# Two edits to the matmul order of a fused attention and two mixtures of experts: a weight maximum moved behind its diagonal, and branches around the slots that may hold no token

## The chip, the cores and the metric

One core of a Trainium2 chip. TensorE (PE) multiplies into PSUM, VectorE (DVE) and ScalarE (ACT) work element by element, GpSimd (POOL) subtracts and issues the scatters by index, SyncE (SP) issues the other DMAs. Each engine runs its own instructions in order and waits for the others by semaphores. The metric is the device time of one execution in microseconds; lower is better.

## The reference

```python
def _attn_ref(u, v, z):                       # batch 4, 2496 tokens, 256 wide, z 64 wide
    scores = (1.0 / S) * np.matmul(z, z.transpose(0, 2, 1))
    return u * np.matmul(np.maximum(scores, 0.0) ** 2, v)

def _moe_ref(x, w_gate, w_output_gate, w1, w2):   # 9984 tokens, 8 experts, 1024 hidden
    logits = x @ w_gate; e_idx = np.argmax(logits, axis=1)
    # gate_w: the chosen expert's softmax probability; eom: sigmoid(x @ w_output_gate)
    for e in range(E):
        mask = e_idx == e
        out[mask] = gate_w[mask, None] * eom[mask, e, None] * (np.maximum(x[mask] @ w1[e], 0.0) @ w2[e])
```

`reference` is the attention, then this first mixture of experts (MoE), then a second one of the same shape without the output gate. How many tokens go to an expert is known only while the kernel runs.

## The kernel before

**Slots.** A MoE gathers its tokens by expert into tiles of 128 rows. There are 9984 = 78 x 128 tokens, and each of 8 experts may leave a last tile part empty, so the program holds 85 slots (`SLOTS`), enough for any split. The first 64 are taken in 32 pairs of full tiles; slots 64 to 84 are single tiles. Three maps (a, b and c) are computed on the chip by `map_stages`: for each unit the row at which its tokens start and the offset of its expert's weights. PE and SP load these numbers into registers (`want_pe`, `get_sp`). A slot past the last tile has expert number 8: the offset is clamped to a valid expert, its rows are padding rows, and its scatter has only indices out of bounds, which write nothing.

**Steps.** A slot has two products. `g1` (x times W1) makes `hp`, from which ACT (relu, line 1303) and DVE (the rounding rest, line 1304) make HB in two float16 parts. `g2` (HB times W2) makes `yp`. A pair's g1 has two parts of 24 matmuls of 256 columns, a single's g1 is 48 matmuls of 128 columns, and a g2 is 24 matmuls of 256 columns. All add three products of float16 parts. `order`, written out by the loop at line 1558, alternates g1 and g2, with g1 ahead by up to 12 slots. In the first MoE eight g1 stand in a row before the last fifteen g2; in the second the last ten g2 stand alone. `hp` (tag "s") and `yp` (tag "a") have two PSUM buffers each.

**After a g2.** In the first MoE `post1` scales `yp` into a row (DVE maximum, line 1345, and inverse; ACT, line 1347; DVE, line 1350), transposes it by DMA to `xlt`, and three or four steps later PE makes the logits (line 548); per four slots `route2` picks the experts and POOL scatters the rows into the second MoE's region (line 654). In the second MoE `post2` scales on ACT (line 1441) and POOL scatters to the output (line 1442).

**Weights.** Both weight matrices of all experts lie in SBUF in two float16 parts. Each of the 16 matrices of the second MoE is split while the first MoE runs (`weight_pieces` with `offload`, line 392). Its pieces, one per step on 114 places (`spots`, line 1584), are: p0 and p1 (DVE maxima of the two halves, lines 427 and 430; p1 ends with `dg`, named `wd` in the trace, a diagonal of 128 maxima, line 436), nothing, p1b (puts the diagonal into the queue `wmq`), nothing, `first` (DVE reads the maximum over all partitions, then ACT scales and rounds half the matrix, lines 463 and 464, and POOL subtracts, line 471) and `last` (the same for the second half). `flush`, run with p0 of the next matrix, issues POOL's stores of the halves and the load of the matrix after next. The sum over partitions that spreads the maximum is a matmul of ones with the diagonal (`wm_mm`, line 384): the next `g2` puts it ahead of its own matmuls, into columns 256 to 383 of its `yp`.

**From one MoE to the other.** After the last g1 of the first MoE (`touch`, then `w_region_load`, line 1609) SP loads the second MoE's W1, one expert per step; after its last g2 the same is done for W2 (line 1593).

Of the kernel before, what the change touches and what calls it, by code (L numbers as in the profile page):

```python
# [13 lines left out]
I32 = mybir.dt.int32  # L14
# [13 lines left out]
def kernel(  # L28
# [351 lines left out]
        return pieces  # L380

    wmq = deque()

    def wm_mm(dst):
        st, dg = wmq.popleft()
        st["wm"] = dst
        T.matmul(dst, onesb, dg, start=True, stop=True)

# [3 lines left out]
    def weight_pieces(items, wst, wo, eng, offload):  # L392
# [13 lines left out]
        def mk(k):  # L406
            i, e = items[k]
            w = wst[k % 2]
            st = {}

            def half(q):
                o = wo[(2 * k + q) % len(wo)]
                if i % 2 == 0:
                    ov = o.rearrange("p (h f) -> p h f", h=2)
                    return ov[:, 0, :], ov[:, 1, :], w[:, q * F : (q + 1) * F], o
                q2 = FC // 2
                ov = o.rearrange("p (f h d) -> p f h d", f=q2, h=2)
                ws = w.rearrange("p (f d) -> p f d", f=FC)
                return ov[:, :, 0, :], ov[:, :, 1, :], ws[:, q * q2 : (q + 1) * q2, :], o

            H = KD * F // 2

            def p0():
                if not offload:
                    flush()
                st["m"] = sm.tile([P, 2], F32, name=f"wm{i}_{e}", tag="wm")
                V.tensor_reduce(st["m"][:, 0:1], w[:, :H], axis=AX.X, op=ALU.max, apply_absolute_value=True)

            def p1():
                V.tensor_reduce(st["m"][:, 1:2], w[:, H:], axis=AX.X, op=ALU.max, apply_absolute_value=True)  # L430
                if offload:
                    m1 = sm.tile([P, 1], F32, name=f"wx{i}_{e}", tag="wx")
                    dg = sm.tile([P, P], BF16, name=f"wd{i}_{e}", tag="fd", bufs=1)
                    tt(m1, st["m"][:, 0:1], st["m"][:, 1:2], ALU.max)
                    V.tensor_single_scalar(m1.bitcast(I32), m1.bitcast(I32), EXPM, ALU.bitwise_and)
                    V.tensor_scalar(dg, idn, m1, None, ALU.mult)
                    st["dg"] = dg
                    return
                st["m2"] = sm.tile([P, 2], F32, name=f"wr{i}_{e}", tag="wr")
                GP.partition_all_reduce(st["m2"], st["m"], P, bass.bass_isa.ReduceOp.max)  # L440

            def p1b():
                wmq.append((st, st["dg"]))

            def p2s():
                m1 = sm.tile([P, 1], F32, name=f"wy{i}_{e}", tag="wy")
                if offload:
                    if "wm" not in st:
                        wm_mm(mbank[0][:, 12 * E * G : 12 * E * G + P])
                    V.tensor_reduce(m1, st["wm"], axis=AX.X, op=ALU.max)  # L450
                else:
                    flush()
                    tt(m1, st["m2"][:, 0:1], st["m2"][:, 1:2], ALU.max)
                sc = sm.tile([P, 1], F32, name=f"ws{i}_{e}", tag="ws")
                near_inv(sc, m1)
                near_pow2(winv[i][:, e : e + 1], m1)
                V.tensor_single_scalar(sc, sc, 4.0, ALU.mult)  # L457
                st["sc"] = sc

            def phi(q):  # L460
                hi, lo, src, _ = half(q)
                if offload:
                    A.activation(src, src, AF.Copy, scale=st["sc"])  # L463
                    A.activation(hi, src, AF.Copy)  # L464
                else:
                    V.tensor_scalar(hi, src, st["sc"], None, ALU.mult)

            def plo(q):
                hi, lo, src, o = half(q)
                if offload:  # L470
                    GP.tensor_tensor(lo, src, hi, ALU.subtract)  # L471
                else:
                    V.scalar_tensor_tensor(lo, src, st["sc"], hi, ALU.mult, ALU.subtract)
                c = q * WB // 4

                def store():
                    eng.dma_start(wd[i][e][:, c : c + WB // 4], o)

                pend.append(store)
                if q == 1 and k + 2 < len(items):  # L480
                    pend.append(lambda: w_load(k + 2))

            def hl(q):
                phi(q)
                plo(q)

            def last():
                phi(1)
                plo(1)

            def first():
                p2s()
                hl(0)

            def none():
                pass

            if offload:
                return (p0, p1, none, p1b, none, first, last)
            return (p0, p1), (p2s, lambda: phi(0), lambda: plo(0)), (lambda: phi(1), lambda: plo(1))  # L500

        ms = [mk(k) for k in range(len(items))]
# [1 line left out]
        none = (0.0, lambda: None)  # L504
        if offload:
            pieces = [(0.0, lambda: w_load(0)), none, none, (0.0, lambda: w_load(1)), none]
            for m in ms:
                pieces += [(0.0, flush)] + [(0.0, f) for f in m]
                pieces[-len(m) - 1 : -len(m) + 1] = [(0.0, lambda p0=m[0]: (flush(), p0()))]
            return pieces + [(0.0, flush)]  # L510

        cost = (1.14, 1.14), (0.8, 0.67, 1.2), (0.67, 1.2)

# [179 lines left out]
    def cumsum(key, x):  # L693
        c = sm.tile([P, E], F32, name=f"cu{key}", tag="cu")
        V.tensor_tensor_scan(c, x, x, 0.0, ALU.add, ALU.bypass)
        return c

    def map_stages(key, m, add, tk, s0, ns, width, done):
        st = {}

# [21 lines left out]
        def f2():  # L722
# [8 lines left out]
            vd = sm.tile([P, 1], F32, name=f"vd{key}", tag="vd")  # L731
            V.tensor_single_scalar(vd, es, float(E), ALU.is_lt)
            tt(tile_i, tile_i, vd, ALU.mult)
            mp = sm.tile([P, 2], F32, name=f"mp{key}", tag="mp")
            V.tensor_single_scalar(mp[:, 0:1], es, float(CAP), ALU.mult)
            V.scalar_tensor_tensor(mp[:, 0:1], tile_i, float(P * width), mp[:, 0:1], ALU.mult, ALU.add)
            V.tensor_scalar(mp[:, 1:2], es, float(E - 1), float(WB), ALU.min, ALU.mult)
# [2 lines left out]
        def f3():  # L740
            mq = mslot("mq")
            st["mq"] = mq
            for c in range(2):
                T.matmul(mq[0:1, c * P : c * P + P], st["mp"][:, c : c + 1], idn, start=True, stop=True)

        def f4():
            mrow = cp.tile([1, 2, ns], I32, name=f"mr{key}", tag=f"mr{key}")
            V.tensor_copy(mrow, st["mq"][0:1, : 2 * P].rearrange("o (c s) -> o c s", c=2)[:, :, :ns])
            done(mrow, st)
            if wready[m]:  # L750
                factors(key, m, st["es"], s0, ns, width)
            else:
                fwait.append(lambda: factors(key, m, st["es"], s0, ns, width))
# [418 lines left out]
    pe_off = {}  # L1172
    sp_row = {}

    UNITS = [2 * i for i in range(NPR)] + list(range(2 * NPR, SLOTS))

    def slot_map(m, s):
# [14 lines left out]
    def want_pe(m, s):  # L1192
        if s < SLOTS and (m, s) not in pe_off and (m, s) not in eoff2 and mapped(m, s):
# [8 lines left out]
            )  # L1202
            for d in range(k):
                pe_off[(m, s + d * width)] = vals[d]

    def get_sp(m, s):
        if (m, s) not in sp_row:
# [71 lines left out]
    def g1(m, s, width, part):  # L1279
# [9 lines left out]
        fn = FC // width  # L1289
        f0 = part * fn  # L1290
        hp = ps.tile([P, 2, 512], F32, name=f"hp{m}_{s}_{part}", tag="s").rearrange("p a b -> p (a b)")
        for f in range(fn):
            rr = [wreg(e, arena0 + W1O + 254 + (kk * F + (f0 + f) * P) * 2) for kk in range(2 * KD)]
            o = hp[:, f * n : (f + 1) * n]
            for k in range(KD):
                xh, xl = T.lower_ap(x[:, k, :]), T.lower_ap(x[:, KD + k, :])
                mm_reg(o, reg_ap(rr[2 * k], P, W1F), xh, k == 0, False)
                mm_reg(o, reg_ap(rr[2 * k], P, W1F), xl, False, False)
                mm_reg(o, reg_ap(rr[2 * k + 1], P, W1F), xh, False, k == KD - 1)
        hpv = hp[:, : fn * n].rearrange("p (f t) -> p f t", t=n)  # L1300
        hv = hb[:, 0, f0 : f0 + fn, :]
        lv = hb[:, 1, f0 : f0 + fn, :]
# [3 lines left out]
    def g2(m, s):  # L1306
# [1 line left out]
        i, h, _ = hslot.pop((m, s))  # L1308
        hfree.append((i, h))
        yp = ps.tile([P, 512], F32, name=f"yp{m}_{s}", tag="a")  # L1310
        if wmq:
            wm_mm(yp[:, D : D + P])
        for f in range(FC):
            rh = wreg(e, arena0 + W2O + f * 4 * D)
            rl = wreg(e, arena0 + W2O + f * 4 * D + 2 * D)
            hi = T.lower_ap(HB[i][:, 0, f, h * P : h * P + P], for_matmul_weights=True)
            lo = T.lower_ap(HB[i][:, 1, f, h * P : h * P + P], for_matmul_weights=True)
            mm_reg(yp[:, :D], hi, reg_ap(rh, D, W2F), f == 0, False)
            mm_reg(yp[:, :D], hi, reg_ap(rl, D, W2F), False, False)
            mm_reg(yp[:, :D], lo, reg_ap(rh, D, W2F), False, f == FC - 1)  # L1320
        return yp

    lgq = deque()
# [229 lines left out]
    for m in range(2):  # L1553
# [42 lines left out]
        touched2 = False  # L1596
        for at, o in enumerate(order):
            kind, s = o[:2]
            if wload:
                wload.popleft()()  # L1600
            if kind == "g1":
# [9 lines left out]
            else:  # L1611
# [3 lines left out]
                    touched2 = True  # L1615
                yp = g2(m, s)
                want_pe(m, next((q[1] for q in order[at + 1 :] if q[0] == "g1" and q[3] == 0), SLOTS))
                if m == 0:
                    post1(s, yp)
                else:  # L1620
                    post2(s, yp)
# [53 lines left out]
```

## Time and profile before

| | us |
|---|---|
| median of 3 runs (1705.81 to 1709.58) | 1708.35 |
| the profiled execution | 1695.75 |
| its span, first to last instruction | 1693.9 |

| engine | busy us | share | instructions |
|---|---|---|---|
| PE (matmuls) | 1627.4 | 96% | 15668 |
| DVE | 1103.2 | 65% | 2805 |
| ACT | 934.2 | 55% | 1082 |
| POOL | 391.4 | 23% | 385 |

The span falls into attention (to about 704 us), the first MoE (to 1232) and the second MoE (to 1694). Busy time counts an engine's own work, not its waits, branches or register loads. "Idle before" is the time in which an engine had nothing running, and "<-" names the instruction that ended it. "issue" means that the profile shows nothing that it waited for.

### The profile page before, as it was taken

The page shows a single profiled execution, that of the slowest core. Times are in us where ns is not written, and L with a number is a line of the kernel's source. Part 1 is how long each engine was busy: PE and PEld are TensorE (multiplying, and loading weights), DVE is VectorE, ACT ScalarE, POOL GpSimd, SP SyncE. Part 2 cuts the span into 40 slices and gives each one's busy share as a digit, 9 for nine tenths or more (in the row PEclk, how much of TensorE's full clock was granted, in tenths as well). Part 3 has the DMA queues.
Part 4 walks back from the last instruction along what each step waited for, and adds up shares of the span by engine and source line. Part 5 has one row for each costly group of instructions (what it writes and reads, how often), then busy time and mean ns, then how long its engine had stood idle before and what let it go on. Part 6 is the DMA issues. An engine that isn't in the chain of part 4 may idle for free. (4 is left out here: it accounts for less than half of the span.)

```text
span 1693.9 us, 41656 instructions
## 1 busy us (share of the span) xinstructions
PE 1627.4 (96%) x15668; PEld 1350.4 (80%) x15668; DVE 1103.2 (65%) x2805; ACT 934.2 (55%) x1082; POOL 391.4 (23%) x385
## 2 busy tenths in 40 slices
PE   8999999999999999989899899889989999999998
PEld 6777677767776777778788778789878888889997
DVE  8799899989999898656666766675463222222221
ACT  8898899889988998422344344443132222222221
POOL 1011111121111221111344344443121111111113
PEclk9999999999999999999999999999999999999999
DMA  5441643363534446962685568653892222222210
GB/s 147 122 110 44 192 101 90 115 202 101 133 99 143 140 138 183 286 167 62 179 186 167 159 157 175 159 141 87 248 275 60 67 51 51 51 51 52 52 33 30
DMA packets 289518, 212.05 MB, mean 125 GB/s; under 512 B 232297, under 2 KB 261358, under 8 KB 284976
## 3 DMA queue, kind: packets, MB, share of 16 engines
q1 hardware_dynamic: 268432, 144.51, 35.5%
q0 software_dynamic: 20896, 64.89, 11.6%
q8 instruction: 134, 2.20, 0.5%
q14 instruction: 56, 0.46, 0.1%
HBM read 92.80 MB, written 69.30 MB: 96 GB/s over the span
## 5 line engine op out<-in xcount | busy, mean ns | idle before, releaser
L1041 PEld LDWEIGHTS <-p 128*128 128x128 f16 (+1 forms) x4644 | 443.8, 98 | 105.3 <-issue 40.2
L1151 PE MATMUL yp<-W2R,HB 128*128 x4080 | 485.4, 278 | 0.1
L1151 PE MATMUL hp<-xt,W1R 128*128 128x256 f16 (+1 forms) x5088 | 475.4, 252 | 9.4 <-DMA xt<-region 3.9
L1151 PEld LDWEIGHTS <-HB 128*128 128x128 f16 x4080 | 403.8, 100 | 88.7 <-issue 36.4
L1304 DVE SCALAR_TENSOR_TENSOR HB<-hp,HB 128x1024 f16<-128x1024 f32 x170 | 207.8, 1223 | 385.2 <-ACT HB L1303 384.8
L1151 PEld LDWEIGHTS <-W1R 128*128 x5088 | 413.0, 98 | 46.1 <-issue 7.0
L1303 ACT ACTIVATE HB<-hp 128x1024 f16<-128x1024 f32 x170 | 173.4, 1021 | 246.3 <-PE hp L1151 236.4
L1041 PE MATMUL acc<-vhA,p 128*128 128x256 f16 (+1 forms) x2322 | 271.1, 273 | 3.6 <-DVE p L151 1.6
L1041 PE MATMUL acc<-vhB,p 128*128 128x256 f16 (+1 forms) x2322 | 270.6, 273 | 0.6 <-ACT acs L1051 0.6
L151 DVE TENSOR_TENSOR p<-r,p 128x1024 f16<-128x1024 f32 (+4 forms) x260 | 244.7, 954 | 36.6 <-ACT p L1006 33.8
L998 ACT ACTIVATE r<-s 128x1024 f32<-128x1024 f32 (+1 forms) x200 | 198.7, 994 | 56.2 <-PE s L987 48.0
L999 ACT ACTIVATE r<-r 128x1024 f32<-128x1024 f32 (+1 forms) x200 | 207.2, 1036 | 6.4
L654 POOL DMA_INDIRECT region<-rowb,pi x80 | 100.1, 1252 | 399.2 <-DVE pi L645 380.9
L1006 ACT ACTIVATE p<-r 128x1024 f16<-128x1024 f32 (+1 forms) x180 | 186.3, 1035 | 5.1
L1442 POOL DMA_INDIRECT out_dram<-rowb,oi x85 | 83.5, 983 | 348.0 <-ACT rowb L1441 342.4
L1347 ACT ACTIVATE rowb<-yp,yg 128x256 f16<-128x256 f32 x85 | 40.1, 472 | 223.2 <-DVE yg L167 187.4
L654 POOL DMA_INDIRECT region<-rowb,piq x85 | 85.0, 1000 | 208.3 <-DVE piq L641 64.7
L1441 ACT ACTIVATE rowb<-yp,cs 128x256 f32<-128x256 f32 x85 | 40.3, 474 | 143.2 <-PE yp L1151 136.3
L471 POOL TENSOR_TENSOR woB<-wstB,woB 128x1024 f16<-128x1024 f32 x32 | 68.1, 2133 | 100.6 <-ACT woB L464 100.5
L1350 DVE SCALAR_TENSOR_TENSOR rowb<-yp,yg,rowb 128x256 f16<-128x256 f32 x85 | 41.1, 483 | 54.5 <-ACT rowb L1347 53.8
L1345 DVE TENSOR_REDUCE gm<-yp 128x1 f32<-128x256 f32 x85 | 35.5, 418 | 27.5 <-PE yp L1151 27.4
L463 ACT ACTIVATE wstB<-wstB,ws 128x1024 f32<-128x1024 f32 x32 | 36.6, 1143 | 30.1 <-DVE ws L457 30.1
(266 smaller groups left out, 1159.1 us busy)
## 6 DMA issues: line engine op xcount, KB each, us to landing
wstA<-in_moe_w_dram SPq DMA_DIRECT2D x16, 1024.0 KB
wsplit<-woA SPq DMA_DIRECT2D x32, 512.0 KB
W1R<-wsplit SPq DMA_DIRECT2D x16, 1024.0 KB
W2R<-wsplit SPq DMA_DIRECT2D x16, 1024.0 KB
wstB<-in_moe_w_dram POOLq DMA_DIRECT2D x16, 1024.0 KB, 8.9
wsplit<-woB POOLq DMA_DIRECT2D x32, 512.0 KB, 4.8
u<-in_u_dram SPq DMA_DIRECT2D x16, 512.0 KB
vraw<-in_v_dram SPq DMA_DIRECT2D x3, 2432.0 KB
```

What stands on the lines that cost most here:

```text
L151: V.tensor_tensor(o, a, b, op)
L471: GP.tensor_tensor(lo, src, hi, ALU.subtract)
L654: d = GP.indirect_dma_start(reg[m], bass.IndirectOffsetOnAxis(ap=posi[:r, t : t + 1], axis=0), rows[:r, t, :], None, bounds_check=NROW - 1 ...
L998: A.activation(r[:, :, :W], s[:, :, :W], AF.Relu)
L999: A.activation(r[:, :, :W], r[:, :, :W], AF.Square, scale=2.0)
L1006: A.activation(p[:, 0, :, :W], r[:, :, :W], AF.Copy)
L1041: T.matmul(o, l, r, start=first and i == 0, stop=j == NT - 1 and i == len(mms) - 1, skip_group_check=True,)
L1151: T.add_instruction(mybir.InstMatmult(name=nc.get_next_instruction_name(), ins=[rhs, lhsT], outs=[T.lower_ap(o)], start_tensor_calc=start, ...
L1303: A.activation(hv, hpv, AF.Relu)
L1304: V.scalar_tensor_tensor(lv, hpv, 0.0, hv, ALU.max, ALU.subtract)
L1350: V.scalar_tensor_tensor(r16[:, q, D : 2 * D], yp[:, :D], yg, r16[:, q, :D], ALU.mult, ALU.subtract)
L1442: d = GP.indirect_dma_start(out, bass.IndirectOffsetOnAxis(ap=ot[:, q : q + 1], axis=0), y, None, bounds_check=N - 1, oob_is_err=False,)
```

## The change

Three things are edited.

1. `wmq` takes the diagonal at the end of p1, with the step from which it may be used (p1's step plus four). `g2` runs `wm_mm` behind its own matmuls, and only from that step on. p1b is gone, `first` comes one piece later, `flush` runs with p1, and `last` is run by the step that holds p0 of the next matrix, behind p0. The cycle stays seven pieces.
2. The maps carry a third number per unit: 1 if the unit holds tokens. The transposing matmuls use 64 columns of the identity each instead of 128.
3. In the last six slots of each MoE (79 to 84) `g1` and `g2` load that flag into a PE register and branch on it. With tokens PE runs the same matmuls as before; without, a filler of four (`g1`) or one (`g2`) matmuls of 256 columns that write finite numbers. Nothing else of a slot is skipped: ACT, DVE, POOL and the DMAs work on it as before. The flags are loaded in two groups of three, behind the g2 of slots 64 and 66.

```diff
     def wm_mm(dst):
-        st, dg = wmq.popleft()
+        _, st, dg = wmq.popleft()
...
-                    st["dg"] = dg
+                    wmq.append((at_item[0] + 4, st, dg))
                     return
...
-            def p1b():
-                wmq.append((st, st["dg"]))
...
-                return (p0, p1, none, p1b, none, first, last)
+                return (p0, p1, none, none, none, none, first, last)
...
-            for m in ms:
-                pieces += [(0.0, flush)] + [(0.0, f) for f in m]
-                pieces[-len(m) - 1 : -len(m) + 1] = [(0.0, lambda p0=m[0]: (flush(), p0()))]
-            return pieces + [(0.0, flush)]
+            steps = [list(m[:7]) for m in ms] + [[]]
+            for k, m in enumerate(ms):
+                steps[k][1] = lambda p1=m[1]: (flush(), p1())
+                if k:
+                    steps[k][0] = lambda lo=ms[k - 1][7], p0=m[0]: (p0(), lo())
+                steps[k] = [(0.0, f) for f in steps[k]]
+                pieces += steps[k]
+            return pieces + [(0.0, ms[-1][7]), (0.0, flush)]
...
+            mp = sm.tile([P, 3], F32, name=f"mp{key}", tag="mp")
+            V.tensor_copy(mp[:, 2:3], vd)
...
-            for c in range(2):
-                T.matmul(mq[0:1, c * P : c * P + P], st["mp"][:, c : c + 1], idn, start=True, stop=True)
+            for c in range(3):
+                T.matmul(mq[0:1, c * MS : c * MS + MS], st["mp"][:, c : c + 1], idn[:, :MS], start=True, stop=True)
...
+    GUARD = SLOTS - 6
...
+    def used_pe(m, s):
+        if (m, s) not in pe_used:
+            key, i, n, _ = slot_map(m, s)
+            k = min(3, n - i)
+            _, vals = nc.values_load_multi_w_load_instructions(
+                ma[key][0][0:1, 2, i : i + k],
+                engines=[ET.PE],
...
+    def guarded(m, s, dst, body):
+        if s < GUARD:
+            body()
+            return
+        with tc.If(used_pe(m, s) > 0) as cmp:
+            body()
+        with cmp.Else():
+            for c in range(0, dst.shape[1], 2 * P):
+                T.matmul(dst[:, c : c + 2 * P], ones, bcm(triu, 2), start=True, stop=True)
...
+        guarded(m, s, hp[:, : fn * n], body)
...
-        if wmq:
-            wm_mm(yp[:, D : D + P])
...
+            if wmq and at_item[0] >= wmq[0][0]:
+                wm_mm(yp[:, D : D + P])
+
+        guarded(m, s, yp[:, :D], body)
...
+            at_item[0] = at
...
+                if s in (2 * NPR, 2 * NPR + 2):
+                    used_pe(m, GUARD + 3 * (s // 2 - NPR))
```

`body` in `g1` and `g2` holds the matmuls that stood there before, unchanged.

## Rows read from the trace of the kernel before

**Rows 1.** The page: section 1 and the instruction queue of section 3.

```profile
PE 1627.4 (96%) x15668; PEld 1350.4 (80%) x15668; DVE 1103.2 (65%) x2805; ACT 934.2 (55%) x1082; POOL 391.4 (23%) x385
...
q8 instruction: 134, 2.20, 0.5%
```

**Rows 2.** Windows, two stages: length, busy PE, PEld, DVE, ACT, POOL, clock, DMA share, GB/s.

```profile
816.70:1140.20 323.50, 293.97 (x3006) 260.60 (x3006) 223.57 (x636) 138.65 (x177) 146.83 (x139) 0.97 0.67 163
...
1271.00:1693.90 422.90, 416.54 (x4311) 378.50 (x4309) 108.06 (x284) 115.78 (x159) 83.55 (x85) 1.00 0.22 50
```

**Rows 3.** Waits, 816.7 to 1140.2: us in total, times, longest us.

```profile
DVE HB L1304 <- ACT HB L1303: 48.6, 28, 3.5
...
DVE rowb L1350 <- ACT rowb L1347: 36.4, 51, 2.2
...
PE yp L387 <- DVE wd L436: 30.1, 12, 4.3
...
ACT HB L1303 <- PE hp L1151: 10.8, 7, 2.1
...
DVE gm L1345 <- PE yp L1151: 4.5, 5, 1.5
```

**Rows 4.** The tile wd: duration ns min/median/max, first and last start us.

```profile
L436 DVE TENSOR_SCALAR wd<-idn,wx x16: 285/286/2762, 816.4 to 1139.9; 128x128 bf16<-128x128 f32 x16
```

**Rows 5.** DVE by line, 816.7 to 1140.2: busy us, mean ns, idle before.

```profile
L427 DVE TENSOR_REDUCE wm<-wstB 128x1 f32<-128x1024 f32 x15 | 18.1, 1210 | 0.0
...
L436 DVE TENSOR_SCALAR wd<-idn,wx 128x128 bf16<-128x128 f32 x15 | 9.1, 608 | 0.5
```

**Rows 6.** Timeline, ACT and DVE at 995: start, us, [idle before <-releaser].

```profile
994.65 1.15 ACT L463 ACTIVATE wstB<-wstB,ws 128x1024 f32<-128x1024 f32 x1 [1.12 <-DVE ws L457]
...
995.88 1.06 ACT L464 ACTIVATE woB<-wstB 128x1024 f16<-128x1024 f32 x1
...
996.84 1.00 ACT L1303 ACTIVATE HB<-hp 128x1024 f16<-128x1024 f32 x1
...
997.88 1.23 DVE L1304 SCALAR_TENSOR_TENSOR HB<-hp,HB 128x1024 f16<-128x1024 f32 x1 [3.26 <-ACT HB L1303]
```

**Rows 7.** The page: section 6, the weight loads of POOL's queue.

```profile
wstB<-in_moe_w_dram POOLq DMA_DIRECT2D x16, 1024.0 KB, 8.9
```

**Rows 8.** Waits, 800 to 1160: DVE for a weight load.

```profile
DVE wm L427 <- DMA wstB<-in_moe_w_dram: 2.6, 1, 2.6
```

**Rows 9.** Line L1196, the register loads of PE's sequencer: ns min/median/max.

```profile
L1196 PEldq TENSOR_LOAD <-mrc x12: 307/1001/1171, 1072.7 to 1653.9; - x12
```

**Rows 10.** Timeline of PE, from one MoE to the other.

```profile
1215.54 0.25 PE L548 MATMUL mbank<-ghl,xlt 128*128 128x16 f16 x4 [1.75 <-DMA xlt<-rowb]
...
1233.06 2.78 PE L1151 MATMUL hp<-xt,W1R 128*128 128x256 f16 x24 [1.15 <-issue]
```

**Rows 11.** Windows of the last slots' scatters; the last column is GB/s.

```profile
1682.50:1685.00 2.50, 2.50 (x26) 2.24 (x24) 0.16 (x1) 0.36 (x2) 0.98 (x1) 1.00 0.01 0
1685.00:1687.50 2.50, 2.50 (x24) 2.04 (x21) 0.00 (x0) 0.43 (x1) 0.98 (x1) 1.00 0.01 0
```

**Rows 12.** Timeline of all engines, the end of the second MoE.

```profile
1655.88 2.84 PE L1151 MATMUL hp<-xt,W1R 128*128 128x128 f16 x48
...
1658.56 28.98 PE L1151 MATMUL yp<-W2R,HB 128*128 x264
...
1685.71 0.98 POOL L1442 DMA_INDIRECT out_dram<-rowb,oi  x1 [1.64 <-ACT rowb L1441]
```

**Rows 13.** Timeline of POOL: scatters that follow each other closely.

```profile
1002.00 1.00 POOL L654 DMA_INDIRECT region<-rowb,piq  x1 [0.30 <-issue]
1003.32 0.98 POOL L654 DMA_INDIRECT region<-rowb,piq  x1 [0.30 <-issue]
```

**Rows 14.** Timeline of DVE: its passes over one yp of the first MoE.

```profile
1231.54 0.42 DVE L1345 TENSOR_REDUCE gm<-yp 128x1 f32<-128x256 f32 x1 [0.76 <-PE yp L1151]
...
1232.69 0.48 DVE L1350 SCALAR_TENSOR_TENSOR rowb<-yp,yg,rowb 128x256 f16<-128x256 f32 x1 [0.54 <-ACT rowb L1347]
```

More of the change, by code (lines that the diff above doesn't have):

```diff
@@ L382 @@
     wmq = deque()
+    at_item = [0]
     def wm_mm(dst):
-        st, dg = wmq.popleft()
+        _, st, dg = wmq.popleft()
         st["wm"] = dst
@@ L696, in cumsum @@
         return c
+    MS = 64
     def map_stages(key, m, add, tk, s0, ns, width, done):
@@ L733, in f2 @@
             tt(tile_i, tile_i, vd, ALU.mult)
-            mp = sm.tile([P, 2], F32, name=f"mp{key}", tag="mp")
+            mp = sm.tile([P, 3], F32, name=f"mp{key}", tag="mp")
+            V.tensor_copy(mp[:, 2:3], vd)
             V.tensor_single_scalar(mp[:, 0:1], es, float(CAP), ALU.mult)
@@ L742, in f3 @@
             st["mq"] = mq
-            for c in range(2):
-                T.matmul(mq[0:1, c * P : c * P + P], st["mp"][:, c : c + 1], idn, start=True, stop=True)
+            for c in range(3):
+                T.matmul(mq[0:1, c * MS : c * MS + MS], st["mp"][:, c : c + 1], idn[:, :MS], start=True, stop=True)
         def f4():
-            mrow = cp.tile([1, 2, ns], I32, name=f"mr{key}", tag=f"mr{key}")
-            V.tensor_copy(mrow, st["mq"][0:1, : 2 * P].rearrange("o (c s) -> o c s", c=2)[:, :, :ns])
+            mrow = cp.tile([1, 3, ns], I32, name=f"mr{key}", tag=f"mr{key}")
+            V.tensor_copy(mrow, st["mq"][0:1, : 3 * MS].rearrange("o (c s) -> o c s", c=3)[:, :, :ns])
             done(mrow, st)
@@ L1204, in want_pe @@
                 pe_off[(m, s + d * width)] = vals[d]
+    pe_used = {}
+    def used_pe(m, s):
[5 more added lines that the diff above has]
+                engines=[ET.PE],
+                min_val=0,
+                max_val=1,
+                skip_runtime_bounds_check_because=SAFE,
+            )
+            for d in range(k):
+                pe_used[(m, s + d)] = vals[d]
+        return pe_used[(m, s)]
+    def guarded(m, s, dst, body):
[7 more added lines that the diff above has]
+                T.matmul(dst[:, c : c + 2 * P], ones, bcm(triu, 2), start=True, stop=True)
     def get_sp(m, s):
@@ L1291, in g1, with body @@
         hp = ps.tile([P, 2, 512], F32, name=f"hp{m}_{s}_{part}", tag="s").rearrange("p a b -> p (a b)")
[L1292 to L1299, printed above, removed]
+        def body():
+            for f in range(fn):
+                rr = [wreg(e, arena0 + W1O + 254 + (kk * F + (f0 + f) * P) * 2) for kk in range(2 * KD)]
+                o = hp[:, f * n : (f + 1) * n]
+                for k in range(KD):
+                    xh, xl = T.lower_ap(x[:, k, :]), T.lower_ap(x[:, KD + k, :])
+                    mm_reg(o, reg_ap(rr[2 * k], P, W1F), xh, k == 0, False)
+                    mm_reg(o, reg_ap(rr[2 * k], P, W1F), xl, False, False)
+                    mm_reg(o, reg_ap(rr[2 * k + 1], P, W1F), xh, False, k == KD - 1)
+        guarded(m, s, hp[:, : fn * n], body)
         hpv = hp[:, : fn * n].rearrange("p (f t) -> p f t", t=n)
@@ L1310, in g2, with body @@
         yp = ps.tile([P, 512], F32, name=f"yp{m}_{s}", tag="a")
-        if wmq:
-            wm_mm(yp[:, D : D + P])
[L1313 to L1320, printed above, removed]
+        def body():
+            for f in range(FC):
+                rh = wreg(e, arena0 + W2O + f * 4 * D)
+                rl = wreg(e, arena0 + W2O + f * 4 * D + 2 * D)
+                hi = T.lower_ap(HB[i][:, 0, f, h * P : h * P + P], for_matmul_weights=True)
+                lo = T.lower_ap(HB[i][:, 1, f, h * P : h * P + P], for_matmul_weights=True)
+                mm_reg(yp[:, :D], hi, reg_ap(rh, D, W2F), f == 0, False)
+                mm_reg(yp[:, :D], hi, reg_ap(rl, D, W2F), False, False)
+                mm_reg(yp[:, :D], lo, reg_ap(rh, D, W2F), False, f == FC - 1)
+            if wmq and at_item[0] >= wmq[0][0]:
+                wm_mm(yp[:, D : D + P])
+        guarded(m, s, yp[:, :D], body)
         return yp
```

## The prediction

> **What bounds the kernel now.** I read the page's section 1 first: PE is busy for 1627.4 us of the 1693.9 us span [rows 1]. That is a mean, so the windows by stage come next [rows 2]. In the second MoE, from 1271 us on, PE is busy 416.54 of 422.90 us and DVE 108.06: PE alone sets the pace. In the part of the first MoE that also splits the second MoE's weights (816.7 to 1140.2 us), PE is busy 293.97 of 323.50 us at a mean granted clock of 0.97. The waits of this stretch [rows 3] name one wait of PE that matters, 30.1 us in 12 times for `wd`, the diagonal that the change gives more time.
>
> The reader should look at the same view from the other side: who waits for PE? DVE waits 4.5 us for `yp`, ACT 10.8 us for `hp`. DVE's long waits are for ACT: 48.6 us for HB and 36.4 us for `rowb`. DVE's busy time and these two make 223.6 + 48.6 + 36.4 = 308.6 of 323.5 us. DVE and ACT, both in order, hand work to each other for 95% of the stretch. Much of PE's wait is therefore time in which this pair catches up.
>
> **1. The weight maximum's matmul.** Before, it stands at the head of a g2, three or four steps behind p1; now at the end of a g2, four or five steps behind p1. `wd` takes 286 ns (2762 ns when disturbed) [rows 4] behind a 1.21 us reduce [rows 5]; a step is about 2.7 us, so the wait itself goes: 30.1 us. [...]
>
> [...]
>
> What is late next? `yp` has two buffers, so a g2 needs DVE's second pass over the `yp` of two g2s before, and `first` must have read the maximum from it. DVE and ACT then pace PE, and only what the pair gains counts. (a) Its idle time for PE: 4.5 us directly, and of the 28 waits for HB 7 had ACT waiting for PE, a quarter of 10.8: together about 7 us. (b) p0 of the next weight now goes ahead of `last` instead of behind it. One of the waits that this fills is in [rows 6]: 3.26 us of DVE behind ACT's two passes (1.15 + 1.06) and HB (1.00). Where `first` follows a g1, the 1.21 us reduce lies in such a wait whole; where it follows a g2, it shortens only a wait for `rowb` (0.7 us on average, 2.2 at most [rows 3]), by an estimated 0.4 us. Eight of each give 13 us. (c) Against it: `flush` goes with p1, and p0 comes one step earlier, so a weight's load has six steps in place of seven; it lands 8.9 us after its issue (median) [rows 7] and stands in POOL's queue behind scatters and subtractions. DVE waited for one once, 2.6 us [rows 8]. I take 4 us, between nothing and 2.6 us for each of 15 loads (39 us). (d) `wd` is slowed when POOL's subtraction runs: 608 ns on average against 286 [rows 4, 5], 4.8 us in all. It may double or go; I take 2 us of loss. Sum: 7 + 13 - 4 - 2 = **14 us** gained, between 0 and 39.8. The piece list grows from 118 to 119 on the same 114 places, which adds no step.
>
> **2. The map.** A third matmul (three of 64 columns for two of 128) and one [128x1] copy on DVE in six maps, known many steps before they are used: 0, at most 6 x 0.15 us.
>
> **3. Flags into PE's registers.** Four more loads. A load holds PE's sequencer for about 1.0 us [rows 9]; 12 of the kind stand in the single tiles of both MoEs, and in the second PE still has its 416.54 of 422.90 us. The sequencer runs that far ahead of the array: 0, and 4 x 1.15 us if it did not (the longest such gap of PE, [rows 10]).
>
> **4. The branches.** 24 guarded blocks (6 slots, two products, two MoEs): a compare at the head, a jump over the other arm. No row has a branch. If the sequencer's lead covers them as it covers the loads: 0. If each cost the longest gap that PE shows for its own issue, 1.15 us: 27.6 us. The load of [rows 9] is the nearest, a longer instruction that is covered, so near the lower end: 0.15 us each, **3.6 us** lost.
>
> [...]
>
> **5. The end of the second MoE.** Are slots empty? The windows at the end move 0 GB/s where the scatters of the last slots are due [rows 11]: slots 82 to 84 hold no token. Counting experts over the reference's inputs gives 82 tiles of 85 in both MoEs. A single tile's g1 takes 2.68 us (1655.88 to 1658.56), a g2 28.98 / 11 = 2.63 us, and a 256-column matmul 28.98 / 264 = 0.11 us [rows 12]. Three g1 become four fillers each: 3 x (2.68 - 0.44) = 6.7 us. DVE and ACT have room (108 and 116 of 423 us [rows 2]), so all of it counts. Three g2 at the very end become one filler each, 3 x 2.63 = 7.9 us. But then POOL's scatters are late next: they still run (0.98 us each in the empty slots too [rows 12]) and follow each other in 1.3 us at the closest [rows 13]: 3 x 1.3 = 3.9 us is exposed. Sum: 6.7 + 4.0 = **10.7 us**, between 6.7 and 14.6.
>
> **6. The end of the first MoE.** Three g1 again save 6.7 us, but here DVE has 1.2 us for HB, 1.6 us for each g2's `yp` (1231.54 to 1233.17 [rows 14]) and about 1 us of routing in a pair that shrinks to 3.1 us: 2 us are lost to it, 4.7 stay. For the last three g2 (2.7 us each with the logits between) DVE's 1.6 us for each `yp` holds the two buffers, and the logits wait for their transposes, which stand behind W1's reload (PE waited 1.75 us for one at 1215.54 [rows 10]). Of 8.2 us I keep 4, less 0.7 us for W2's reload, which fills the queues right behind. **8 us**, between 3 and 14.
>
> **The sum** against the profiled execution, 1695.75 us (span 1693.9 and 1.85 around it): 14 + 10.7 + 8 - 3.6 = 29.1, so 1666.7 us. The median of the runs shown is 1708.35, 12.6 us above that execution; on its scale 1708.35 - 29.1 = **1679 us**, 1.7% faster.
>
> **Rivals.**
> - *PE was the bound of the weight stretch.* [...] For it: PE shows no other wait there. Against: hardly anyone waits for PE. [...]
> - *The wait only moves.* PE stops at `yp` for as long as it stopped at `wd`, and the loads eat (a) and (b): part 1 is 0, the rest 15.1: 1693 us. For it: the pair is taken 95%.
> - *The branches drain PE: slower.* At each of the 24 blocks the jump loses the code that was fetched, and PE restarts from nothing. The price from rows: an instruction packet's time, 0.5% of 16 engines' span over 134 packets [rows 1] = 1.0 us, and the 1.15 us of a start from the sequencer: 2.15 x 24 = 51.6 us against a gain of 32.7: 1727 us. It decides from 1.4 us a block. Against it: both targets lie close ahead, and a covered 1.0 us is already shown.
> - *The fillers are not reached* (flags always set): 14 - 3.6: 1698 us. The 0 GB/s speaks against it.
>
> [...]
>
> **How the numbers follow.** Forecast 0.50, PE-bound 0.18, wait only moves 0.17, branches drain 0.12, fillers not reached 0.03. The range 1652 to 1703 takes in all but the slower case and leaves some for it and for a gain above the ceiling: about 8 in 10. A measurement tells about 0.2% (3.4 us) from no change. Faster: 0.50 + 0.18 + 0.17 + 0.03, less 0.06 for smaller gains met by dearer branches, 0.82; within 0.2%: 0.05; slower: 0.13.
>
> **What would show it.** In the weight stretch PE's wait for `wd` gone, and in its place waits of PE for DVE or ACT at `yp` or `hp`; DVE's waits for ACT shorter by some 10 us; the stretch some 14 us shorter. At both ends three g1 of 4 and three g2 of 1 matmul; the last real g2 followed by three scatters 1.3 us apart. Around the 24 blocks gaps of PE below 0.3 us. The prediction is wrong if the stretch shrinks by over 25 us (PE was the bound) or by under 5, or if guarded blocks with tokens take over 3 us.

## The result, and the profile after

The change makes the kernel faster: median 1666.47 us of four runs (1661.74 to 1670.73) against 1708.1 us of four runs of before; ratio 0.9757, 95% interval 0.9723 to 0.9791. The forecast was 1679, its range 1652 to 1703. The profiled execution of after takes 1663.35 us (span 1661.5); the one of before took 1695.75 (span 1693.9). So the profiles differ by 32.4 us and the medians by 41.6; the experiments take up that difference, but do not settle all of it.

First the page of the kernel after, its section 1 and the instruction queue, which answer to [rows 1]:

```profile
PE 1596.2 (96%) x15278; PEld 1320.4 (79%) x15278; DVE 1095.2 (66%) x2811; ACT 933.8 (56%) x1082; POOL 391.1 (24%) x385
...
q8 instruction: 135, 2.21, 0.5%
```

PE does 31.2 us less, and instruction fetches did not grow (134 packets before). The windows of after for the two stages of [rows 2], the weight stretch from its first to its last `wd` matmul, and the second MoE from its first g2 to the end:

```profile
813.20:1123.70 310.50, 289.36 (x3009) 258.40 (x3007) 218.76 (x645) 140.72 (x179) 146.75 (x139) 0.99 0.74 170
1249.60:1661.50 411.90, 402.34 (x4111) 364.88 (x4110) 108.19 (x285) 115.45 (x159) 83.50 (x85) 0.99 0.23 51
```

The second MoE is 11.0 us shorter between these bounds (422.90 before). The bounds of the weight stretch are not the same slots any more, since the matmul moved. Measured between fixed points, from DVE's first pass over the `yp` of slot 16 to that of slot 68, it took 323.4 us before and 307.1 after. Now the waits in it, as in [rows 3] (total us, times, longest us):

```profile
DVE HB L1341 <- ACT HB L1340: 35.3, 23, 5.3
...
DVE rowb L1391 <- ACT rowb L1388: 27.4, 46, 2.2
...
PE mbank L550 <- DVE Lq L555: 5.7, 3, 2.3
PE yp L1156 <- issue: 3.7, 5, 1.1
PE mbank L749 <- DVE mpa L742: 3.1, 1, 3.1
PE mbank L550 <- issue: 3.0, 3, 2.0
PE hp L1156 <- issue: 2.2, 2, 1.2
...
DVE wm L428 <- DMA wstB<-in_moe_w_dram: 4.3, 3, 2.3
```

PE's wait for `wd` (30.1 us) is gone, but for one of 0.8 us. PE now waits for other products of DVE, though not for `yp` or `hp` as I had written: for `Lq`, which frees the bank of the logits, and for the map. The largest part of what is left, 8.9 us in ten gaps, has no releaser in the profile ("issue"; 0.3 us before). It does not belong to the change: w_only, flags_on and after_again, which have the same weight pieces, show 1.9 to 2.0 us of it between the same slots. Its cause is not known. DVE's waits for ACT fell from 48.6 and 36.4 us to 35.3 and 27.4. Its wait for a weight load rose from nothing to 4.3 us: the 2.6 us of [rows 8] stand at 812.5 us, ahead of the stretch. The pass that makes `wd`, as in [rows 5] (busy us, mean ns, idle before):

```profile
L437 DVE TENSOR_SCALAR wd<-idn,wx 128x128 bf16<-128x128 f32 x16 | 5.2, 322 | 0.6
```

It is no longer slowed (608 ns on average before, where two of the 16 passes took 2.76 and 2.63 us, each beside a subtraction of POOL of 2.14 us; in after none of the 16 lies beside one). The register loads of PE's sequencer, old and new, as in [rows 9] (ns min/median/max):

```profile
L1202 PEldq TENSOR_LOAD <-mrc x12: 305/1002/2872, 1052.4 to 1627.8; - x12
L1218 PEldq TENSOR_LOAD <-mrc x4: 764/780/2573, 1093.8 to 1595.2; - x4
```

Then the branches and the fillers: PE's timeline in the second MoE, around the first guarded slots with tokens and the three without (start, us, what, idle before):

```profile
1605.10 2.78 PE L1156 MATMUL yp<-W2R,HB 128*128 x24
1607.72 2.84 PE L1156 MATMUL hp<-xt,W1R 128*128 128x128 f16 x48
1610.40 2.78 PE L1156 MATMUL yp<-W2R,HB 128*128 x24
...
1621.00 2.78 PE L1156 MATMUL yp<-W2R,HB 128*128 x24
1623.62 0.60 PE L1237 MATMUL hp<-triu,ones 128*128 128x256 f16 x4
1624.06 2.78 PE L1156 MATMUL yp<-W2R,HB 128*128 x24
...
1651.13 0.27 PE L1237 MATMUL yp<-triu,ones 128*128 128x256 f16 x1
1651.92 0.27 PE L1237 MATMUL yp<-triu,ones 128*128 128x256 f16 x1 [0.52 <-ACT rowb L1482]
1652.37 0.27 PE L1237 MATMUL yp<-triu,ones 128*128 128x256 f16 x1 [0.18 <-ACT rowb L1482]
```

The g1 at 1607.72 is the first behind a branch: 2.62 us lie between it and the start ahead of it, 2.68 to the next, with no idle time in the record. A filler g1 takes 0.44 us instead of 2.68. Behind the last real g2 the scatters remain, in POOL's timeline:

```profile
1652.08 0.98 POOL L1483 DMA_INDIRECT out_dram<-rowb,oi  x1 [1.64 <-ACT rowb L1482]
1653.36 0.98 POOL L1483 DMA_INDIRECT out_dram<-rowb,oi  x1 [0.30 <-ACT rowb L1482]
1654.65 0.98 POOL L1483 DMA_INDIRECT out_dram<-rowb,oi  x1 [0.30 <-issue]
1655.94 0.98 POOL L1483 DMA_INDIRECT out_dram<-rowb,oi  x1 [0.30 <-issue]
```

They stand 1.28 to 1.29 us apart, as in [rows 13], and three of them are exposed: nothing else runs while they do.

### The profile page after: what moved, and what is told of

It reads as the page before. It is cut to its first block, busy times and chain, and to the rows that moved or that the text cites. A ratio compares the mean times of both kernels' runs of the same rounds, so it can differ in the third digit from the quotient of the medians.

```text
span 1661.5 us, 40789 instructions
## 1 busy us (share of the span) xinstructions
PE 1596.2 (96%) x15278; PEld 1320.4 (79%) x15278; DVE 1095.2 (66%) x2811; ACT 933.8 (56%) x1082; POOL 391.1 (24%) x385
## 5 line engine op out<-in xcount | busy, mean ns | idle before, releaser
L1156 PE MATMUL hp<-xt,W1R 128*128 128x256 f16 (+1 forms) x4800 | 465.4, 255 | 13.2 <-issue 8.2
L1156 PE MATMUL yp<-W2R,HB 128*128 x3936 | 456.9, 273 | 4.8 <-issue 4.0
L1156 PEld LDWEIGHTS <-W1R 128*128 x4800 | 399.5, 99 | 55.2 <-issue 17.6
L1156 PEld LDWEIGHTS <-HB 128*128 128x128 f16 x3936 | 383.8, 98 | 52.5 <-issue 7.3
L1391 DVE SCALAR_TENSOR_TENSOR rowb<-yp,yg,rowb 128x256 f16<-128x256 f32 x85 | 41.1, 484 | 51.1 <-ACT rowb L1388 41.0
L550 PEld LDWEIGHTS <-xlt 128*128 128x128 f16 x660 | 29.1, 97 | 34.3 <-issue 18.1
```

Source lines behind the costliest of these rows:

```text
L1156: T.add_instruction(mybir.InstMatmult(name=nc.get_next_instruction_name(), ins=[rhs, lhsT], outs=[T.lower_ap(o)], start_tensor_calc=start, ...
L1391: V.scalar_tensor_tensor(r16[:, q, D : 2 * D], yp[:, :D], yg, r16[:, q, :D], ALU.mult, ALU.subtract)
```

## Experiments

Twelve more runs were made, in three jobs of four; each job was on another chip and has its own runs of before. Medians and ratios come from the runs; the stages are read from each kernel's profiled execution. A is slot 16 to slot 68 of the first MoE, B slot 68 to the first g2 of the second MoE (the end of the first MoE with both reloads), C from ACT's pass over the `yp` of slot 64 of the second MoE to the end. A difference between stages of two runs compares two single executions, mostly on two chips.

```
kernel         A      B      C     median   before   ratio (95%)
before       323.4  126.4  85.5   1708.1
after        307.1  125.6  74.7   1666.47  1708.1    0.9757 (0.9723-0.9791)
w_only       308.2  126.6  85.5   1675.85  1698.41   0.9875 (0.9854-0.9895)
g_only       323.3  123.0  74.7   1678.71  1698.41   0.9891 (0.9874-0.9909)
flags_on     306.6  126.7  85.5   1675.54  1698.41   0.9868 (0.9842-0.9894)
short_max    292.7  124.3  74.7   1643.77  1698.41   0.9691 (0.9668-0.9714)
late_only    316.5  122.9  74.7   1669.49  1707.37   0.9780 (0.9757-0.9804)
order_only   336.7  124.6  74.7   1691.79  1707.37   0.9897 (0.9873-0.9922)
g1_m0        309.5  128.0  74.7   1672.05  1707.37   0.9794 (0.9770-0.9817)
no_w1_reload 308.0  119.8  74.7   1660.14  1707.37   0.9732 (0.9709-0.9755)
before_again 322.5  132.9  85.5   1697.09  1695.45   1.0005 (0.9991-1.0018)
after_again  308.2  121.0  74.7   1658.14  1695.45   0.9769 (0.9750-0.9787)
late_again   316.1  123.4  74.7   1668.59  1695.45   0.9835 (0.9815-0.9856)
w1_on_act    306.9  141.2  74.7   1672.83  1695.45   0.9858 (0.9840-0.9877)
```

**w_only: the weight part without the guards.**

```diff
-    GUARD = SLOTS - 6
+    GUARD = SLOTS
...
-                if s in (2 * NPR, 2 * NPR + 2):
-                    used_pe(m, GUARD + 3 * (s // 2 - NPR))
```

> Only the weight part of the change: no slot is guarded, no flag is loaded into a register (the flags are still computed in the map). Theory A (the pair of DVE and ACT is relieved, and only a part of PE's wait is a gain): the stretch from slot 16 to slot 68 of the first MoE takes about 307 us as in the changed kernel (323.4 before), everything behind it runs as before, so the profiled execution lies 16 to 22 us under the one of before (the first stage moved by 4 us too, which I put down to chance or to the loads of W2, and this run tells which). Rival B (PE was the bound of the stretch): the gain is near 40 us and the guards cost what is missing. Rival C (only the guards gain): no change, within 4 us.

Stage A came to 308.2 us and the profiled execution (1674.97) lies 20.8 us under that of before: theory A. Of these, 15.2 us lie in stage A and 5.7 ahead of slot 16. 40 us (B) and 4 us (C) are out. The few us of the early stage are taken up under "What stays open".

**g_only: the guards with before's weight pieces.** The edit takes back every line of the diff in the weight pieces and in the place of `wm_mm`.

> Only the guards: the weight maximum has its old place and the old order of the pieces. Theory A: 10.7 us at the end of the second MoE (6.7 from three g1, 4.0 from three g2), about 1 us at the end of the first one, nothing lost to branches: 11 to 13 us under before. Rival (the branches cost something, 1 us or more for each of the 24 blocks): at most no change, up to 15 us slower. The weight stretch takes 323 us, as before.

Stage C is 10.8 us shorter, A unchanged (323.3), B 3.4 shorter; the profiled execution is 16.1 us under that of before, the median 19.7 under before's. That is more than theory A, and far from the rival: the branches cost nothing that shows.

**flags_on: every flag 1.**

```diff
-            V.tensor_copy(mp[:, 2:3], vd)
+            V.memset(mp[:, 2:3], 1.0)
```

> The changed kernel with every flag set to 1, so that all 24 guarded blocks run their matmuls and no filler is reached; compare and branch are all executed. Theory A (branches are covered by the sequencer's lead): the time of the run with the weight part alone, within 2 us, and gaps of PE at the heads of guarded blocks below 0.3 us. Rival (a branch costs 0.15 us, my term): 3.6 us more than that run. Rival (a branch drains PE, 2.15 us a block): 50 us more.

Medians 1675.54 and 1675.85 without any branch: equal within their spread (1669.66 to 1680.56, 1673.35 to 1677.52). The windows of the second MoE say it more sharply. First flags_on, then w_only, each from the first g2 to the end:

```profile
1252.00:1674.70 422.70, 416.35 (x4313) 378.56 (x4311) 108.10 (x285) 115.65 (x159) 83.57 (x85) 1.00 0.23 50
```

```profile
1250.40:1673.10 422.70, 416.33 (x4313) 378.54 (x4311) 108.19 (x285) 115.78 (x159) 83.58 (x85) 1.00 0.21 50
```

With twelve guarded blocks or none the stage takes 422.70 us. To the 0.1 us of these windows the branches cost nothing; both rivals fall.

**short_max: a cheaper maximum.** Both reduces read 64 columns in place of 1024, so most of the maximum is left out.

```diff
-    V.tensor_reduce(st["m"][:, 0:1], w[:, :H], ...)
+    V.tensor_reduce(st["m"][:, 0:1], w[:, :64], ...)
```

> The changed kernel with both reduces of a second-MoE weight's maximum over 64 columns in place of 1024 (it leaves out most of the maximum, so the scale is another). DVE loses about 2 x 1.06 us of work for each of 16 weights, 34 us in the stretch. Theory A (the pair of DVE and ACT still bounds the weight stretch): the stretch of slots 16 to 68 shrinks from 307 us by 8 to 20 us more, PE alone would need about 286. Rival B (PE or the loads bound it by now): it stays within 3 us.

Stage A shrank from 307.1 to 292.7 us. Its window:

```profile
815.70:1108.40 292.70, 282.85 (x3008) 254.96 (x3007) 198.87 (x638) 139.50 (x177) 146.99 (x139) 1.00 0.80 180
```

The two reduces of a weight took 36.3 us there in after and take 6.3 now, by DVE's lines:

```profile
L428 DVE TENSOR_REDUCE wm<-wstB 128x1 f32<-128x64 f32 x15 | 3.2, 213 | 3.5 <-DMA wstB<-in_moe_w_dram 3.5
L431 DVE TENSOR_REDUCE wm<-wstB 128x1 f32<-128x64 f32 x15 | 3.1, 209 | 0.0
```

DVE's busy time fell by only 17 of these 30 us (215.84 to 198.87; some small instructions became slower, as `vl` from 468 to 743 ns), and the stretch by 14.4. With less work on DVE PE is idle for 9.9 us (21.1 in the same window of after) and its clock reaches 1.00. Theory A holds: in the changed kernel the pair still bounded this stretch, PE did not. For the kernel before that is argued from its waits, not tried.

**late_only and late_again: the matmul late, the old order of the pieces.** The matmul goes to the end of the same g2 whose head it had; nothing else of the weight part changes.

```diff
-        if wmq:
-            wm_mm(yp[:, D : D + P])
...
+            if wmq and at_item[0] >= wmq[0][0]:
+                wm_mm(yp[:, D : D + P])
```

> The changed kernel with the old order of the pieces: only the place of the weight maximum's matmul differs from before, at the end of the same g2 instead of its head (it is ready 2.6 us longer). By my working the wait itself is worth (a) 7 us of the weight stretch (slots 16 to 68: 323.4 before, 307.0 with both parts), so about 316 us, and the run lies some 8 us above the changed kernel. Rival (the wait was the whole matter, the order of the pieces nothing): 307 us and the changed kernel's time. Rival (the order is everything): 322 us.

> The late matmul alone with the old order of the pieces, a second time, now beside the whole change on one chip. Theory A (the order of the pieces brings something once the wait is gone, as the profile of 316.5 us against 307 says): stretch 314 to 318 us, the median 6 to 10 us above the whole change. Rival B (the order brings nothing, as the medians 1669.5 and 1672.0 of the last job say): the medians agree within 2 us.

Stage A took 316.5 and 316.1 us. On one chip the run lies 10.4 us above the whole change (1668.59 against 1658.14), just over the 6 to 10 us of theory A of the second text. The medians of the job before do not agree: late_only stands 2.6 us under g1_m0, which has all of the weight part and lacks only fillers worth some 3.3 us (below), so that the order would be worth 0.7 us there. In the profiles of that job stage A is 7.0 us shorter in g1_m0, but its slot 16 comes 5.7 us later. Stage A speaks for the order on both chips, the medians on one. PE's waits in stage A of late_again:

```profile
PE yp L388 <- DVE wd L437: 9.0, 7, 2.5
PE mbank L549 <- DVE Lq L554: 7.1, 5, 1.8
```

Of 27.8 us of waiting between the same two points before, 19 are gone, and the stretch is only 6.0 to 7.3 us shorter than in the three profiles with the old pieces: what PE no longer waits for here it waits for at other places. The windows of the stage, in before, late_again and after:

```profile
821.30:1144.70 323.40, 293.89 (x3011) 260.58 (x3008) 223.54 (x636) 138.65 (x177) 146.83 (x139) 0.97 0.67 162
818.80:1134.90 316.10, 294.26 (x3033) 261.75 (x3031) 223.71 (x637) 138.31 (x177) 147.13 (x139) 0.97 0.71 166
816.80:1123.90 307.10, 286.02 (x2980) 255.57 (x2978) 215.84 (x637) 139.33 (x177) 146.75 (x139) 0.99 0.75 171
```

With the matmul late PE is idle for less time, but its busy time and its clock (0.97) stay as they were. Both change only with the new order.

**order_only: the new order, the matmul at its old place.** The entry is due at `at_item[0] + 3` and stands again at the head of the g2.

> The changed kernel with the matmul at the head of the g2, as far behind p1 as before: only the order of the pieces differs from before (p0 of the next weight ahead of last). By my working this is (b) 13 us less (c) 4 and (d) 2: the stretch takes about 316 us with PE still waiting for wd. Rival (the wait was the whole matter): 322 us. Rival (the order is everything): 308 us.

All three theories missed: stage A takes 336.7 us in a profiled execution (1695.58) that is the longest of its runs (from 1684.38). Its ratio to before (0.9897) is that of g_only (0.9891), which has the same guards and the old order; its median is 13.1 us above that of g_only, on another chip. Alone, the order brings nothing, and in that profile it costs 13 us. Its window, and under it its wait for `wd`:

```profile
820.60:1157.30 336.70, 301.13 (x3005) 263.20 (x3003) 221.45 (x638) 140.19 (x177) 146.73 (x139) 0.94 0.70 156
```

```profile
PE yp L388 <- DVE wd L437: 23.6, 8, 5.0
```

PE waits 3.0 us each time (27.8 us in 11 times, 2.5 each, between these points before) and its granted clock falls to 0.94: PE's busy time rises by 7.2 us for the same matmuls. A likely reason, argued and not tried: `first`, `last`, p0 and p1 now stand on three steps instead of four, so that `wd` comes later to a matmul that is not later.

**g1_m0: second products of the first MoE unguarded.**

```diff
-        guarded(m, s, yp[:, :D], body)
+        if m == 0:
+            body()
+        else:
+            guarded(m, s, yp[:, :D], body)
```

> The changed kernel with the second products of the first MoE unguarded (its last three g2 run their 24 matmuls; nine guarded products fewer to branch at is not the point). Theory (the last three g2 of the first MoE lie beside waits for DVE and for the transposes behind W1's reload, so their fillers gain nothing): the same time as the changed kernel within 2 us, from slot 70 to the second MoE's start about 91 us in both. Rival (my term, 4 us for them): 4 us slower.

The stretch took 92.4 us against 90.0 in after and 87.8 in after_again, and the part from slot 79 to the touch of the second MoE's W1 18.1 us, against 14.4 to 15.1 in the seven profiles with all guards and both reloads unchanged. (The edit takes the branch from six products, not from nine as the text has it.) So the three g2 fillers of the first MoE gain some 3.3 us: my theory of that moment, drawn from one pair of profiles, was wrong, and the term of the prediction right.

**no_w1_reload: the second MoE without its own W1.**

```diff
-                    w_region_load(W1R, 2)
```

> The changed kernel without the second load of W1, so that the second MoE runs with the first one's W1 (the output is another). Theory (at the end of the first MoE the transposes of the last tiles and with them the logits stand behind this load in the DMA queues): the stretch from slot 70 to the second MoE's start, 90.0 us in the changed kernel and 91.3 before, shrinks to 83 to 86 us, and PE's waits for transposes of up to 3.8 us go. Rival (DVE's chain for the tiles and the routing sets this end): 89 us or more.

From slot 70 it took 83.4 us: the theory. PE's waits for transposes between slot 68 and the touch of the second MoE's W1, first in after, then in this kernel:

```profile
PE mbank L550 <- DMA xlt<-rowb: 9.0, 6, 3.8
```

```profile
PE mbank L550 <- DMA xlt<-rowb: 3.1, 3, 1.2
```

These waits fell by 5.9 us. Stage B is 5.8 us shorter than in after and 3.7 shorter than the mean of those seven profiles (123.5): the reload costs about that, and the waits for transposes cover it.

**w1_on_act: the reload from another queue.**

```diff
-            wload.append(lambda e=e: w_load_one(Q, dst, i, e))
+            wload.append(lambda e=e: w_load_one(A if i == 2 else Q, dst, i, e))
```

> The changed kernel with the eight loads of W1's reload issued from ACT's DMA queue instead of SP's, where the transposes of the last tiles go too. Theory A (the transposes wait in line behind the 1 MB loads of their own queue): slot 70 to the second MoE's first second product takes 84 to 87 us in place of 90.0, PE's waits for transposes at this end shrink, and the run is 3 to 6 us faster than the changed kernel. Rival B (the loads and the transposes share the same 16 DMA engines, which are 88% busy there, whatever the queue): 89 us or more, no change. Rival C (ACT is held at the loads and PE waits for its HB): slower by some us.

The run is 14.7 us slower than after_again, and for a reason that none of the theories had. From slot 70 it took 107.9 us in a profile (1680.51) that is the longest of its runs. PE does not wait there for an HB that ACT holds up, as rival C had it, but longer for the transposes: 20.6 us in place of 9.0. PE's wait for them as above, then the DMA queues from slot 70 to that touch (packets, MB, share of 16 engines; q10 is ACT's):

```profile
PE mbank L550 <- DMA xlt<-rowb: 20.6, 5, 9.6
```

```profile
q10 hardware_dynamic: 1152, 8.39, 48.2%
q1 hardware_dynamic: 8707, 1.99, 46.5%
```

In the kernel after one queue carries both in this part:

```profile
q1 hardware_dynamic: 9778, 10.37, 84.2%
```

Summed over the packets and shared among 16 engines that is 84.2% of 46.3 us, 39 us, for 10.4 MB; from two queues the packets of the same bytes take 94.7% of 66 us, 62.5 us. Here sharing the queue is the better of the two; why the packets take longer was not tried.

**before_again and after_again: both kernels on one chip, with profiles.** Unchanged files.

> The kernel before, unchanged, for a profile of it on the same chip as the three others. Its one profiled execution so far (1695.75 us) lies 12.6 us under the median of its own runs there (1708.35), and on three chips its medians are 1708, 1698 and 1707. Theory A (the difference between executions lies in the weight stretch, whose waits come out otherwise each time): slots 16 to 68 take 323 to 335 us here, and the long runs are those with the long stretch. Rival B (the scatter lies elsewhere, in the stage ahead of the first MoE or at the wait for W2): the stretch takes 323.4 us as in both profiles of the old order of pieces.

> The changed kernel, unchanged, beside before on one chip: slots 16 to 68 in 306.6 to 309.5 us as in five profiles with the same weight pieces, slot 70 to the second MoE's first second product in 90 us, the ratio to before near 0.976.

Stage A is 322.5 us here, and 323.4 and 323.3 in the two other profiles of the old pieces; with the new ones it was 306.6 to 309.5 in seven. It hardly scatters, so theory A of the first text falls. Stage B scatters: 126.4 and 132.9 us in the same kernel, 121.0 and 125.6 in the changed one. From slot 70 after_again took 87.8 us, not the 90 expected. On this chip the medians differ by 37.3 us, the profiles by 41.1: A 14.3, B 11.9, C 10.8, and 4 us elsewhere, ahead of slot 16.

## Why the prediction was right, and where not

- **The size.** The sum was 29.1 us against the profiled execution, so 1666.7; it took 1663.35. The forecast for the median was 12.5 us too long, because I carried over the 12.6 us by which before's median stood above its profile. That gap belonged to before alone: after's profile is 3.1 us under its median, and before's own medians in two of the three later jobs (1695.45 and 1698.41) lie close to the profile shown. That step of the working failed. From job to job before's median moved by 13 us (1695 to 1708). That the sum came within 3.3 us of the profile is in part luck: this pair differs by 16.3 us in A, 0.8 in B (8 predicted), 10.8 in C and 4.5 ahead of slot 16, where nothing was predicted, and the 3.6 us for branches were not spent.
- **1, the weight part: 14 predicted, 15 measured** (three profiles with the old pieces average 323.1, seven with the new 307.8). The main reason held: PE's wait was mostly time in which DVE and ACT caught up, since 19 us less waiting gave 6.8 (late) and 30 us less of reduces another 14 (short_max). DVE's waits for ACT fell by 22 us in after and 16 in w_only, where I had some 10. (a) was 7 and measured 6.8. (b) to (d) were 13 - 4 - 2 = 7 and measured 8.5, but only on top of (a): I had added two parts that are not independent, for alone the order gives nothing. Within it (c) was 4.3 us in after and 8.5 in w_only (I took 4; before has no such wait between these slots), and (d) had the wrong sign: `wd` went from 608 to 322 ns, 4 us gained for DVE. PE's next wait for DVE came at `Lq`, not at `yp` or `hp`.
- **The first rival's share.** Between the same slots PE's busy time averages 293.4 us in the three profiles with the old pieces and 288.2 in the seven with the new, at a granted 0.97 and 0.98 to 0.99; its idle time averages 29.6 and 19.6 us. So about 5 of the 15 us came through the clock. (The first pair alone gives 8, but its trace after holds 31 matmuls fewer, some 3 us.) Late alone brought none of it: its busy time was 293.9 and 294.3 us. Half or more of what the new order adds to it is therefore clock, and not, as (b) has it, only time of DVE that p0 fills; the last waits for `wd` go with the new order, and no run separates the two. Where the clock was low the trace of before shows: behind six of the twelve waits of PE for `wd`, of 2.1 to 4.3 us, the g2 took 4.34 to 5.30 us, at a granted 0.50 to 0.57 in 2 us of it; behind the six others, of 0.3 to 3.4 us, it took 2.78. The 39.8 us at the upper end of part 1 are the 30.1 us of the wait and 9.7 us for the clock; no run shows a gain of 9.7 there, and the runs showed about 5 in its place. The rival needed all of the clock and all of the idle time, and 19.6 us of idle time are left.
- **2 and 3, map and register loads: 0 predicted, and none shows.** The four new loads (0.78 us, median) leave no gap at the guarded slots.
- **4, branches: 3.6 predicted, 0 measured** (422.70 us with and without). No run shows the 0.15 us a block that the 3.6 were made of. Four register loads (0.31 to 1.01 us) and the first branches stand in PE's sequencer in after between 1589.7 and 1630 us, and PE has no gap there. The third rival is out: there are 135 packets of instruction fetch against 134. Six fillers in each MoE are reached by taken branches, and ahead of none does PE show a gap without a releaser ("issue"); a target further away was not run.
- **5, the second MoE's end: 10.7 predicted, 10.8 measured**, in its two parts as well: 6.7 for three g1 (2.68 less 0.44 us each), which leaves 4.1 for three g2 with 3 x 1.3 us of scatters exposed.
- **6, the first MoE's end: 8 predicted, about 5 measured** (B averages 128.2 in four profiles in which no filler runs and 123.5 in seven in which all do). Slot 70 to 79 gave 2.8 of the 4.7 I had kept for g1, slot 79 to the touch of W1 3.5 of 4, and the part behind it, with the reload of W2, takes back 1.1 (0.7). One profile of this stage says little: the first pair alone gave 0.8 us.
- **What stays open.** 15 + 11 + 5 = 31 us; the medians of whole runs say 37 to 42. The parts have the same gap: w_only and g_only are 22.6 and 19.7 us under before on their chip, and their stages account for about 15 and 14. Ahead of slot 16 the change adds only the map's column and the first pieces of one weight. Both profiles of before begin the first MoE at 703.9 and 706.2 us, the others at 702.1 to 705.1. From there to slot 16 it took 117.3 and 113.9 us in before and 111.8 to 117.7 in the others, whichever order they had. So this stretch moves by some us without the change; why, and why before's median differs from job to job, was not settled.

## What to carry to other kernels

Before a wait is taken away, ask what its releaser would be late with next: late_only removed 19 us of waiting for 7 us of time, and the rest came only when the releaser's own work was put in another order. A forward branch on PE over one product (24 or 48 matmuls) was free here (422.70 us with twelve guarded blocks and with none), so padding can be skipped by a flag; what then shows is the work that is not guarded, here scatters at 1.3 us each. Compare sums with the profile they were made on, and take a stage's scatter from several profiles before a few us of it are explained.

## What was not expected of the hardware

- Branch and compare on PE: 0 us in a stage of 422.70 us with 12 guarded blocks.
- Large loads and transposes from two DMA queues took 62.5 us of packet time for the bytes that took 39 us from one (one profile each), and a single transpose kept PE waiting for 9.6 us in place of 3.8.
- In the one profile of order_only, with waits for `wd` of 3.0 instead of 2.5 us and 35.6 instead of 29.5 us of idle time, the granted clock of the stretch was 0.94 instead of 0.97, and the same matmuls took 301.1 instead of 293.9 us.
- Taking away two thirds of PE's wait for `wd` (late_only, late_again) left the granted clock at 0.97; it came to 0.98 to 0.99, and in short_max to 1.00, only in the kernels in which that wait was all but gone.
